# A kernel of attention and two MLPs: three narrow chunks beside attention in place of five, and groups of two steps with one tile

## The chip, the cores and the metric

The kernel runs on one core of a Trainium2 chip. The time is the device time of one execution in microseconds (us), the median of three runs; lower is better. Before the change it is 940.36 us (940.23 to 940.99).

## The reference

Three stages follow each other. `x` is the attention's output with the heads side by side, 2304 tokens of 512 values.

```python
# attention with random features: q, k, v (4, 8, 576, 64), omega (128, 64)
def phi(x):
    h = x @ omega.T - sum(x*x)/2          # x scaled before
    h = h - max(h)
    return exp(h) / sqrt(m)
kv  = phi(k).T @ v                         # per head, 128 x 64
z   = sum of phi(k)
out = (phi(q) @ kv) / (phi(q) @ z + 1e-6)
# first MLP: w_in (512, 2048), w_out (2048, 512)
h = x @ w_in
x = (max(h, 0) + alpha * min(h, 0)) @ w_out
# second MLP: w_a, w_b (512, 1536), w_out (1536, 512)
out = ((x @ w_a) * (x @ w_b)) @ w_out
```

## The kernel before

**Stages.** Attention runs in steps. A step takes a piece of 128 tokens (the last of a head group 64) of one group of four heads through its parts: projections `pp` of k and q on TensorE (a_proj), the maximum `nm` on VectorE (a_max), the exponential `ph` on ScalarE (a_exp), the state products `kv` (a_kv, with the copy `kvp` on ScalarE at the end of a head group, L838), the transposition `tp` of q's features and its copy `phT` (a_t, copied at L852 or on VectorE), the numerators `nd` with the reciprocals and quotients `xn` on VectorE (a_num), and the transposition `xp` of the output with its copy `xT` (a_x, at L894 or on VectorE). A part of a step comes some steps after the one it rests on, so that each step of the order holds parts of several pieces.

The first MLP is cut into 16 tiles of d_ff (128 each) in two phases of 8, and the tokens into chunks. A chunk's tile is 12 matmuls `h` (three for each of four slices of d_model, since every fp32 number is a high and a low part, xh and xl, wh and wl), the leaky relu with `u` and the parts `gh` on ScalarE and `gl` on VectorE, and 12 matmuls `y`. The chunks' inputs are split into xh (ScalarE, L517) and xl (L521). The second MLP, with a scheme that spares products (from 526.1 us), is not touched.

**What sets the order.** Every engine's order is written out by hand; a wait in an engine's queue holds all that is behind it. Steps 0 to 14 of attention run alone. From step 15 on (SPLIT_AT) narrow chunks of 256 tokens run beside attention, in the order of `work0`: chunks 0 and 1 in halves (tiles 0 to 4 of chunk 0, of chunk 1, tiles 5 to 7 of chunk 0, of chunk 1), then chunks 2, 3 and 4. At first A.run takes one tile and one step at a time. After ALONE = 4 entries of work0, which is from step 31 on, group() takes over: two steps and two tiles each. When attention has ended the rest of the narrow tiles run in pairs, then come the REST chunks, 512 wide, and the second phase.

Weights arrive packed and are decoded in pieces, through POOL, VectorE and ScalarE (L259 makes `r`, L308 the high part `w` from `a`). D_.step and D_.go set how many pieces stand at a place of the order.

**Banks and buffers.** PSUM has one bank for `kv`, five shared under the tag "ps" by pp, tp, nd, xp and the narrow tiles' h, and two for y. phT and xn have two buffers each, gh and gl three, u two; kvp three.

**Names.** On TensorE `y_256_0` is chunk 256 (its first token), half 0 of the output; `h_512_3` tile 3 of chunk 512; `pp(6, 1)_False` the projections of the keys of head group 6, piece 1 (and of a query's piece beside them; True means queries alone); `kv` a head group's state; `nd_4`, `xp_4`, `tp_4`, `phT_4` a piece 4 of some head group; the number behind is the tensor's own.

Of the kernel before, what the change touches and what calls it, by code (L numbers as in the profile page):

```python
# [23 lines left out]
KT = DM // P  # L24
# [8 lines left out]
WARM = 11  # L33
Q_LAG = 6
CI = 256
NCI = 5
NF0 = 8
NFH = 5
CB = 512
REST = (512, 512)  # L40
CHUNKS = (512, 512, 256, 512, 512)
NS = 25
NS1 = 17
# [9 lines left out]
DEC1 = 1.0  # L53
# [5 lines left out]
PACE2 = 1  # L59
PACE3 = 1  # L60
FIRST = 32
ALONE = 4
LAND = 5.0
SIDE = 0

# [2 lines left out]
def tile_kernel(ctx: ExitStack, tc: tile.TileContext, qT, kT, v1, omT, wbits, alpha, out):  # L68
# [58 lines left out]
    for ph in range(PH2):  # L127
        q = PB + QS * ph
        for j in range(2):
            f = 4 * ph + 2 * j  # L130
            for m in range(2):
                n = q + 7 * j + 3 * m
# [347 lines left out]
    class Mlp:  # L480
        def __init__(self, st, cap, ybufs, side=None):
            self.cap = cap
            self.pair = 2 * cap <= 512
            pool = lambda **kw: st.enter_context(tc.tile_pool(side=side, reuse_waits="tile" if side else "pool", **kw))

            if not self.pair:
                self.px = pool(name=f"px{cap}", bufs=6)
            self.xs, self.ys, self.gs, self.part = {}, {}, {}, {}
            self.half = {}
            self.q = []  # L490
            self.beside = None
            self.seen = set()
            self.after = []
            self.open_ = lambda: self.rest(pool, ybufs)
            if self.pair:
                self.open_()
# [104 lines left out]
        def a_back(self, ph, o, n, f, last_chunk):  # L601
# [23 lines left out]
                if i == end and not self.pair and e < 3 and not last:  # L625
                    D_.fill()
            D_.free[2 * f + 1] = last_chunk
            if last:
                if halves and f == NFH - 1:

                    yh = xT[:, :, 3 * S + o:3 * S + o + n]
                    for e in range(KT):
                        if e % 2:
                            vector.tensor_copy(yh[:, e], ys[e])
                        else:
                            nc.scalar.activation(yh[:, e], ys[e], AF.Copy)
                    self.half[o] = yh
                elif halves:
                    yo = self.half.pop(o)
                    for e in range(KT):  # L640
                        vector.tensor_tensor(out=yo[:, e], in0=ys[e], in1=yo[:, e], op=ALU.add)
                    nc.sync.dma_start(out=ypart[:, :, o:o + n], in_=yo)
                elif ph == 0:
                    yo = self.io.tile([P, KT, self.cap], F32, tag="io", name=f"yo{o}")[:, :, :n]
                    for e in range(KT):
                        if e % 2:
                            vector.tensor_copy(yo[:, e], ys[e])
                        else:
                            nc.scalar.activation(yo[:, e], ys[e], AF.Copy)
                    nc.sync.dma_start(out=ypart[:, :, o:o + n], in_=yo)  # L650
                else:
                    yp = self.part.pop(o)
                    for e in range(KT):
                        vector.tensor_tensor(out=yp[:, e], in0=ys[e], in1=yp[:, e], op=ALU.add)
                    nc.sync.dma_start(out=ypart[:, :, o:o + n], in_=yp)
                self.ys.pop(o)

        def load_y(self, o, n):
            yp = self.io.tile([P, KT, self.cap], F32, tag="io", name=f"yp{o}")[:, :, :n]
# [181 lines left out]
    def a_t(u, t):  # L841

        ns = slots_of(t)
        ph = phiq.pop((u, t))
        pp = bank(f"tp{u}_{t}").rearrange("p (o m) -> p o m", m=P)
        for h in range(ns):
            tensor.transpose(pp[:, h, :], ph[:, h, :], ident)
        d = pq.tile([P, 4, P], F32, tag="phT", name=f"phT{u}_{t}", bufs=2)
        if pick({"act": 0.1 + 0.13 * ns}, {"dve": 0.1 + 0.15 * ns}):
            vector.tensor_copy(d[:, :ns], pp[:, :ns])  # L850
        else:
            nc.scalar.activation(d[:, :ns], pp[:, :ns], AF.Copy)  # L852
        phT[u, t] = d
# [23 lines left out]
    def a_x(u, t, into=None):  # L877

        done["x"].add((u, t))
        b, g = divmod(u, HG)  # L880
        xn = xns.pop((u, t)).rearrange("p (a j) d -> p a (j d)", j=2)
        xp = (bank(f"xp{u}_{t}")[:, :256] if into is None else into).rearrange("p (a n) -> p a n", a=2)
        n = P if t < 4 else 64
        if t < 4:
            for a in range(2):
                tensor.transpose(xp[:, a, :], xn[:, a], ident)
        else:
            tensor.transpose(xp[:, 0, :], xn[:, 0], ident)
            xp = xp[:, 0, :].rearrange("p (a n) -> p a n", a=2)
        dst = xT[:, 2 * g:2 * g + 2, b * S + t * P:b * S + t * P + n]  # L890
        if pick({"act": 0.2 + n / 600}, {"dve": 0.1 + n / 480}):
            vector.tensor_copy(dst, xp)
        else:
            nc.scalar.activation(dst, xp, AF.Copy)  # L894
# [3 lines left out]
    done = {"kv": set(), "x": set()}  # L898
    late = {1: 3, 2: 3, 3: 4, 4: 5}
    own_banks = (0, 3, *range(6, SPLIT_AT, 2))  # L900
    held = {}
    for i, ut in enumerate((u, t) for u in range(U) for t in range(TT)):
        ev["k"][i] = ut
        ev["kv"][i + 1] = ut
# [110 lines left out]
    with st_m:  # L1015
# [38 lines left out]
        def group(fronts, at):  # L1054

            s = nxt_s[0]
            nxt_s[0] += 2
            D_.step(2 * DEC1)
            full = s < last_q
            todo = {n: wait[n][:2] for n in wait}  # L1060
            for n in wait:
                wait[n] = wait[n][2:]
            kv, t = list(todo["kv"]), list(todo["t"])
            for ut in todo["x"]:
                a_x(*ut)
            if kv:
                a_kv(*kv.pop(0))
            for ut in todo["num"]:
                a_num(*ut)
                wait["x"].append(ut)  # L1070
            if kv:
                a_kv(*kv.pop(0))
            spread(fronts, KT)
            A.flush()
            for x in (s, s + 1):
                pj = attn_1(x)
                loads(x)
                if pj:
                    a_exp(*pj, a_max(*pj))
                if x in ev["k"]:  # L1080
                    wait["kv"].append(ev["k"][x])
                if x in ev["q"]:
                    wait["t"].append(ev["q"][x])
            spread(line[at:at + 5], 2)
            D_.go(5)
            for i in range(2):
                if i < len(t):
                    a_t(*t[i])
                    wait["num"].append(t[i])
                if full:  # L1090
                    A.back_one(fronts, 2 - i)
            for w in fronts:
                A.whole(*w)
                if not full:
                    A.back_one(fronts)
            D_.go(3)

        def more():
            return nxt_s[0] < last_q or any(wait.values())
# [22 lines left out]
        def beside(ph, ci, i):  # L1122
# [13 lines left out]
            "num": [ut for ut in queries if ut in phT],  # L1136
            "x": [ut for ut in queries if ut in xns]})

        line = [(ph, o, n, f, lc) for ph, o, n, fs, lc in work0 for f in fs]

        def spread(fronts, most):
# [12 lines left out]
        while i < len(line):  # L1154
# [1 line left out]
                spread(line[i:i + 5], 2)  # L1156
            pair = []
            early = 1 if more() else 0
            for w in line[i:i + 2]:
                ph, o, n, f, _ = w  # L1160
                if all((ph, o, k) in A.xs or x_there(o + n, k, True) for k in range(KT)) and D_.ready >= 2 * f + 2 - early:
                    pair.append(w)
            if len(pair) < 2 and more():
                pair = []
            if more():
                group(pair, i)
            else:
# [6 lines left out]
        A.flush()  # L1174
        while more():
            group([], i)
        over()
        while A.q:
            A.pop()
# [338 lines left out]
```

## Time and profile before

| | |
|---|---|
| median of three runs | 940.36 us (940.23 to 940.99) |
| profiled execution, its own time | 941.56 us |
| its span in the profile | 939.8 us |
| TensorE (PE) busy | 928.4 us, 99% |
| VectorE (DVE) busy | 610.8 us, 65% |
| ScalarE (ACT) busy | 509.5 us, 54% |
| GpSimd (POOL) busy | 126.0 us, 13% |
| PE, h of the first MLP, first high part | 768 matmuls, 189.0 us |
| PE, y, first high part | 768 matmuls, 184.6 us |

The profile is of one execution. Its own time is 1.76 us over its span, and 1.2 us over the median of the runs. PE, DVE, ACT and POOL are the engines; PEld is TensorE's loading of weights, which goes on beside the matmuls. A time of day in the rows is counted in us from the start of the span. The first narrow tile begins at 41.0 us, and the last narrow chunk ends at 241.90 us. The granted clock is TensorE's, as a share of full speed.

### The profile page before, as it was taken

The numbers are of one execution on the slowest core, as the hardware profiler recorded it, in microseconds if no ns is written. First come the engines' busy times: TensorE is split into PE (matmuls) and PEld (weight loads), VectorE is DVE, ScalarE is ACT, GpSimd is POOL, SyncE is SP. The second block draws the span as 40 slices with busy tenths as digits, with TensorE's granted clock in tenths as the row PEclk, the third lists the DMA queues.
The fourth block names the chain that finished last, engine by engine and source line by source line (L and its number), as shares of the span: only waits on it lengthen the run. The fifth ranks groups of instructions, "written<-read, shape, count | busy, mean of one in ns | idle before, by whom it ended". The sixth has DMA issues, their size and how long they took to land.

```text
span 939.8 us, 16686 instructions
## 1 busy us (share of the span) xinstructions
PE 928.4 (99%) x6483; PEld 842.8 (90%) x6483; DVE 610.8 (65%) x1247; ACT 509.5 (54%) x1196; POOL 126.0 (13%) x107
## 2 busy tenths in 40 slices
PE   8899999999999999999999999999999999999998
PEld 7789999999888888889888999999999898989896
DVE  5988775644567677678676796866486833374633
ACT  7878865553455554455444555655456542444541
POOL 3677700000010201000000000000011111010201
PEclk9999999999999999999999999999999999999999
DMA  9354431000234242455555856269727368333323
GB/s 333 132 208 145 149 102 50 24 1 24 90 90 135 88 159 68 167 192 196 202 180 218 309 208 234 82 211 396 285 64 239 64 188 274 102 38 97 56 46 68
DMA packets 49566, 138.92 MB, mean 148 GB/s; under 512 B 4560, under 2 KB 11088, under 8 KB 49488
## 3 DMA queue, kind: packets, MB, share of 16 engines
q1 hardware_dynamic: 44592, 129.08, 38.6%
q0 software_dynamic: 4752, 8.65, 6.4%
q8 instruction: 51, 0.84, 0.3%
q14 instruction: 27, 0.22, 0.1%
q10 hardware_dynamic: 144, 0.13, 0.0%
HBM read 90.66 MB, written 47.19 MB: 147 GB/s over the span
## 4 chain that ended last, share of the span: by engine, by line
PE 95%; ACT 2%; DVE 2%; issue 0%; ACTq 0%; DVEq 0%
PE y L191 21%; PE h L191 21%; PE W L191 16%; PE o L191 16%; PE E L191 8%; PE B L191 4%; PE tp L191 2%; ACT ph L818 2%; PE kv L191 2%; PE nd L191 2%; PE xp L191 1%; DVE xl L521 0%; DVE a L191 0%; PE warm L191 0%; DVE xn L191 0%
## 5 line engine op out<-in xcount | busy, mean ns | idle before, releaser
L191 PE MATMUL h<-xh,w 128*128 128x256 f32 (+1 forms) x768 | 189.0, 338 | 0.4 <-DVE gl L191 0.4
L191 PE MATMUL y<-gh,w 128*128 128x256 f32 (+1 forms) x768 | 184.6, 339 | 0.0
L191 PEld LDWEIGHTS h<-xh,w 128*128 128x128 f32 x768 | 125.8, 190 | 16.0 <-DVE gl L191 0.6
L191 PEld LDWEIGHTS y<-gh,w 128*128 128x128 f32 x768 | 123.3, 189 | 15.1
L191 PE MATMUL o<-w,gh 128*128 128x512 f32 x432 | 133.2, 389 | 0.0
L191 PE MATMUL h<-xl,w 128*128 128x512 f32 (+1 forms) x384 | 109.9, 337 | 0.4 <-DVE xl L521 0.4
L191 PE MATMUL y<-gl,w 128*128 128x512 f32 (+1 forms) x384 | 109.5, 336 | 0.0
L191 PEld LDWEIGHTS o<-w,gh 128*128 128x128 f32 x432 | 81.0, 188 | 16.5
L191 DVE SCALAR_TENSOR_TENSOR h<-u,bend,h 128x512 f32<-128x512 f32 (+1 forms) x72 | 47.8, 663 | 56.9 <-ACT u L555 56.8
L191 PE MATMUL o<-w,gl 128*128 128x512 f32 x216 | 84.2, 390 | 0.0
L1417 POOL DMA_DIRECT2D out<-op x30 | 26.3, 877 | 421.9 <-ACT op L166 339.7
L567 ACT ACTIVATE gh<-h 128x512 fp32r<-128x512 f32 (+1 forms) x72 | 38.0, 527 | 64.7 <-DVE h L191 64.7
L191 PEld LDWEIGHTS h<-xl,w 128*128 128x128 f32 x384 | 64.3, 190 | 8.1 <-DVE xl L521 0.6
L191 PEld LDWEIGHTS y<-gl,w 128*128 128x128 f32 x384 | 64.1, 189 | 7.4
L555 ACT ACTIVATE u<-h 128x512 f32<-128x512 f32 (+1 forms) x72 | 38.1, 529 | 56.2 <-PE h L191 51.7
L521 POOL TENSOR_TENSOR xl<-xT,xh 128x512 fp32r<-128x512 f32 (+1 forms) x16 | 20.2, 1274 | 334.5 <-ACT xh L517 334.5
L166 ACT ACTIVATE u<-W 128x384 f32<-128x384 f32 x72 | 35.3, 492 | 50.6 <-PE W L191 47.3
L166 ACT ACTIVATE op<-o 128x512 f32<-128x512 f32 x51 | 30.4, 597 | 58.2 <-PE o L191 44.8
L191 DVE TENSOR_TENSOR u<-E,u 128x384 f32<-128x384 f32 x36 | 19.6, 555 | 52.5 <-PE E L191 49.7
L191 DVE TENSOR_TENSOR gl<-h,gh 128x512 fp32r<-128x512 f32 (+1 forms) x72 | 43.1, 599 | 15.4 <-ACT gh L567 14.6
L191 DVE CUSTOM_DVE_ANT_0 a<-a,r 128x1024 uint16<-128x1024 uint16 x68 | 49.1, 723 | 4.8 <-ACT r L259 0.8
L191 PEld LDWEIGHTS o<-w,gl 128*128 128x128 f32 x216 | 40.5, 188 | 8.4
(496 smaller groups left out, 1971.9 us busy)
## 6 DMA issues: line engine op xcount, KB each, us to landing
raw<-in_w SPq DMA_DIRECT2D x68, 512.0 KB, 5.1
w<-store SPq DMA_DIRECT2D x45, 512.0 KB, 6.9
store<-t_None SPq DMA_DIRECT2D x40, 512.0 KB, 3.6
st<-ypart SPq DMA_DIRECT2D x14, 768.0 KB, 7.4
out<-op POOLq DMA_DIRECT2D x30, 256.0 KB, 5.4
q<-in_qT SPq DMA_DIRECT2D x8, 576.0 KB, 3.8
v<-in_v SPq DMA_DIRECT2D x7, 650.0 KB, 6.2
yp<-ypart SPq DMA_DIRECT2D x4, 1024.0 KB, 6.3
```

The costliest lines, as they stand in the source:

```text
L166: nc.scalar.activation(out, in_, AF.Copy)
L191: return call(*a, **k)
L521: (nc.vector, nc.gpsimd)[way].tensor_tensor(out=lo, in0=src, in1=hi.bitcast(F32), op=ALU.subtract)
L555: nc.scalar.activation(u_, hp, AF.Relu, scale=-1.0)
L567: nc.scalar.activation(gh, hp, AF.Copy)
L818: nc.scalar.activation(ph[:, 2 * pr + j], pair[j][:, o + pr], AF.Exp, bias=nm[:, j, o + pr:o + pr + 1])
L1417: nc.gpsimd.dma_start(out=dst, in_=op, accum_op=ALU.add)
```

## The change

Of the nine narrow or wide chunks of the first phase, five of 256 and two of 512 tokens become three of 256 and three of 512. Groups begin after the first halves of chunks 0 and 1, with step 25, and hold two steps and one tile. Their parts are in another order, listed from the state products on: kv, nd, xp of both steps, the projections, then y of the tile before, then tp, then h. The maximum comes ahead of what A.flush emits (the rest of the tile before: gh and gl), the exponentials behind it. Within groups the copies phT are all on VectorE and the copies xT all on ScalarE; before, each was put where a running count of load was lower. The pieces of decoding (D_.go) stand behind tp and at the end, and D_.step is given one step's worth a group instead of two. The copies of a finished chunk's y out of PSUM are collected and emitted a little later (leave).

```diff
-NCI = 5
+NCI = 3
-REST = (512, 512)
+REST = (512, 512, 512)
-ALONE = 4
+ALONE = 2
...
@@ a_back
-            if last:
+
+            def leave():
                 if halves and f == NFH - 1:
...
+            if last:
+                self.outs.append(leave)
+                if not self.hold:
+                    self.leave()
+
+        def leave(self):
+            while self.outs:
+                self.outs.pop(0)()
+
@@ a_t
-        if pick({"act": 0.1 + 0.13 * ns}, {"dve": 0.1 + 0.15 * ns}):
+        if grouped or pick({"act": 0.1 + 0.13 * ns}, {"dve": 0.1 + 0.15 * ns}):
             vector.tensor_copy(d[:, :ns], pp[:, :ns])
@@ a_x
-        if pick({"act": 0.2 + n / 600}, {"dve": 0.1 + n / 480}):
+        if not grouped and pick({"act": 0.2 + n / 600}, {"dve": 0.1 + n / 480}):
             vector.tensor_copy(dst, xp)
@@ group
-            D_.step(2 * DEC1)
-            full = s < last_q
+            D_.step(DEC1)
             todo = {n: wait[n][:2] for n in wait}
             for n in wait:
                 wait[n] = wait[n][2:]
-            kv, t = list(todo["kv"]), list(todo["t"])
-            for ut in todo["x"]:
-                a_x(*ut)
-            if kv:
-                a_kv(*kv.pop(0))
+            for ut in todo["kv"]:
+                a_kv(*ut)
             for ut in todo["num"]:
                 a_num(*ut)
                 wait["x"].append(ut)
-            if kv:
-                a_kv(*kv.pop(0))
-            spread(fronts, KT)
-            A.flush()
+            for ut in todo["x"]:
+                a_x(*ut)
             for x in (s, s + 1):
                 pj = attn_1(x)
                 loads(x)
+                nm = a_max(*pj) if pj else None
+                A.flush()
                 if pj:
-                    a_exp(*pj, a_max(*pj))
+                    a_exp(*pj, nm)
...
-            spread(line[at:at + 5], 2)
-            D_.go(5)
-            for i in range(2):
-                if i < len(t):
-                    a_t(*t[i])
-                    wait["num"].append(t[i])
-                if full:
-                    A.back_one(fronts, 2 - i)
+            end = not (more() or todo["t"])
+            if not end:
+                A.back_one(fronts, 1)
+            for ut in todo["t"]:
+                a_t(*ut)
+                wait["num"].append(ut)
+            A.leave()
+            D_.go(3)
+            spread(fronts, KT)
             for w in fronts:
                 A.whole(*w)
-                if not full:
-                    A.back_one(fronts)
-            D_.go(3)
+                A.back_one(fronts)
+            A.leave()
+            spread(line[at:at + 5], 2)
+            D_.go()
...
-            for w in line[i:i + 2]:
+            for w in line[i:i + 1] if more() else line[i:i + 2]:
...
-            if len(pair) < 2 and more():
-                pair = []
```

Three places of the order are shown. The first is TensorE's queue where head group 5 ends and 6 begins. Before:

```order
L191 MATMUL kv_2005<-v_1587,ph_4_2275 64x65 x8
L191 MATMUL nd_1_2398<-kvp_169,phT_1_2310 64x65 x8
L191 MATMUL tp_0_2412<-ident,ph_0_2192 128x128 x4
L191 MATMUL y_256_0_2419<-gh_256_5_2174,w_89 128x256 x4
L191 MATMUL y_256_1_2420<-gh_256_5_2174,w_89 128x256 x4
L191 MATMUL y_256_0_2419<-gl_256_5_2175,w_89 128x256 x2
L191 MATMUL y_256_1_2420<-gl_256_5_2175,w_89 128x256 x2
L191 MATMUL xp_0_2433<-ident,xn_0_2303 128x128 x2
L191 MATMUL xp_1_2437<-ident,xn_1_2410 128x128 x2
L191 MATMUL kv_2441<-v_2088,ph_0_2379 64x65 x8
```

And after the change, the same place:

```order
L191 MATMUL kv_1994<-v_1587,ph_4_2213 64x65 x8
L191 MATMUL kv_2317<-v_2052,ph_0_2236 64x65 x8
L191 MATMUL nd_1_2326<-kvp_169,phT_1_2263 64x65 x8
L191 MATMUL nd_0_2340<-kvp_170,phT_0_2270 64x65 x8
L191 MATMUL xp_4_2354<-ident,xn_4_2172 128x128
L191 MATMUL xp_0_2357<-ident,xn_0_2186 128x128 x2
L191 MATMUL pp(6, 1)_False_2361<-xT,k_1886 128x128
```

The first product of the new head group (kv_2441 before, kv_2317 now) has moved up to directly behind the last of the old one.

The second is ScalarE's queue at the copy kvp_170 of the same place. Before:

```order
L567 ACTIVATE gh_256_7_2360<-h_256_7_2336 128x256
L818 ACTIVATE ph_0_2379<-pp(6, 0)_False_2362,nm(0, 6, 0)_2373 128x128 x2
L818 ACTIVATE ph_2_2380<-pp(6, 0)_False_2362,nm(0, 6, 0)_2373 128x128 x2
L818 ACTIVATE ph_0_2379<-pp(6, 0)_False_2363,nm(0, 6, 0)_2373 128x128 x2
L818 ACTIVATE ph_2_2380<-pp(6, 0)_False_2363,nm(0, 6, 0)_2373 128x128 x2
L838 ACTIVATE kvp_170<-kv_2005 128x260
L894 ACTIVATE xT<-xp_0_2433 128x2x128
L894 ACTIVATE xT<-xp_1_2437 128x2x128
```

After:

```order
L259 ACTIVATE r_2276<-raw_2120 128x512
L588 ACTIVATE u_0_7_2295<-h_0_7_2282 128x256
L518 ACTIVATE xh_512_0_2298<-xT 128x256
L518 ACTIVATE xh_512_1_2302<-xT 128x256
L308 ACTIVATE w_94<-a_2126 128x512
L849 ACTIVATE kvp_170<-kv_1994 128x260
L905 ACTIVATE xT<-xp_4_2354 128x2x64
L905 ACTIVATE xT<-xp_0_2357 128x2x128
L595 ACTIVATE gh_0_7_2374<-u_0_7_2295 128x256
```

In front of kvp_170 stood exponentials; now the u of a tile, two splits and a decoder's instruction stand there.

The third is ScalarE's queue in two of the last groups that hold attention. Before:

```order
L587 ACTIVATE u_1024_2_3860<-h_1024_2_3847 128x256
L587 ACTIVATE u_1024_3_3890<-h_1024_3_3877 128x256
L894 ACTIVATE xT<-xp_4_3905 128x2x64
L594 ACTIVATE gh_1024_2_3908<-u_1024_2_3860 128x256
L594 ACTIVATE gh_1024_3_3912<-u_1024_3_3890 128x256
```

After:

```order
L588 ACTIVATE u_512_4_3332<-h_512_4_3319 128x256
L905 ACTIVATE xT<-xp_3_3363 128x2x128
L905 ACTIVATE xT<-xp_4_3367 128x2x64
L595 ACTIVATE gh_512_4_3370<-u_512_4_3332 128x256
L588 ACTIVATE u_512_5_3404<-h_512_5_3391 128x256
L905 ACTIVATE xT<-xp_2_3417 128x2x128
L905 ACTIVATE xT<-xp_3_3421 128x2x128
L595 ACTIVATE gh_512_5_3425<-u_512_5_3404 128x256
```

Two tiles shared such a passage before, one tile has it to itself now, with two copies xT between its u and its gh.

## Rows read from the trace of the kernel before

**Rows 1.** The page: busy us (share of the span) xinstructions of each engine

```profile
PE 928.4 (99%) x6483; PEld 842.8 (90%) x6483; DVE 610.8 (65%) x1247; ACT 509.5 (54%) x1196; POOL 126.0 (13%) x107
```

**Rows 2.** TensorE's waits from 99 to 242: us in total, times, longest

```profile
PE tp L191 <- DVE xn L191: 0.2, 1, 0.2
```

**Rows 3.** Stretches: length, busy PE, PEld, DVE, ACT, POOL, clock, DMA share, GB/s

```profile
0.00:25.00 25.00, 21.90 (x297) 19.23 (x299) 14.07 (x38) 18.53 (x59) 9.29 (x12) 0.93 0.90 331
132.50:163.85 31.35, 31.35 (x414) 30.28 (x413) 18.80 (x50) 18.54 (x64) 0.00 (x0) 1.00 0.25 83
163.85:241.90 78.05, 77.78 (x870) 75.29 (x869) 39.85 (x120) 37.64 (x115) 0.00 (x0) 1.00 0.05 15
```

**Rows 4.** Timeline of TensorE: start, us, engine, operation, [idle before]; 24 matmuls twice

```profile
227.98 0.64 PE L191 MATMUL h<-xl,w 128*128 128x256 f32 x4
...
230.86 0.64 PE L191 MATMUL h<-xl,w 128*128 128x256 f32 x4
...
402.41 0.39 PE L191 MATMUL y<-gh,w 128*128 128x512 f32 x1
...
407.85 0.39 PE L191 MATMUL y<-gh,w 128*128 128x512 f32 x1
```

**Rows 5.** Timeline of TensorE: beginnings of pieces in steps 25 to 34

```profile
98.98 0.72 PE L191 MATMUL h<-xh,w 128*128 128x256 f32 x4
...
100.59 0.71 PE L191 MATMUL pp(5, 0)_False<-xT,k 64*128 64x128 f32 x8
...
132.53 0.60 PE L191 MATMUL xp<-ident,xn 128*128 128x128 f32 x4
...
142.88 0.69 PE L191 MATMUL kv<-v,ph 128*64 128x65 f32 x16
...
144.90 0.71 PE L191 MATMUL pp(6, 3)_False<-xT,k 64*128 64x128 f32 x8
...
146.66 0.66 PE L191 MATMUL tp<-ident,ph 128*128 128x128 f32 x4
147.07 1.19 PE L191 MATMUL y<-gh,w 128*128 128x256 f32 x8
...
148.58 0.38 PE L191 MATMUL tp<-ident,ph 128*128 128x128 f32 x2
...
153.11 0.60 PE L191 MATMUL xp<-ident,xn 128*128 128x128 f32 x4
153.64 0.69 PE L191 MATMUL kv<-v,ph 128*64 128x65 f32 x16
...
241.90 0.40 PE L191 MATMUL h<-xh,w 128*128 128x512 f32 x1
```

**Rows 6.** Timelines of ScalarE and TensorE: copies and what releases them

```profile
99.33 0.63 ACT L308 ACTIVATE w<-a 128x512 fp32r<-128x512 f32 x1 [0.21 <-DVE a L191]
...
99.87 0.37 ACT L852 ACTIVATE phT<-tp 128x256 f32<-128x256 f32 x1
...
172.37 0.84 ACT L517 ACTIVATE xh<-xT 128x256 fp32r<-128x256 f32 x2
...
185.46 0.69 PE L191 MATMUL kv<-v,ph 128*64 128x65 f32 x16
186.19 0.39 ACT L838 ACTIVATE kvp<-kv 128x260 f32<-128x260 f32 x1 [0.51 <-PE kv L191]
...
227.40 0.27 PE L191 MATMUL xp<-ident,xn 128*128 128x128 f32 x1
227.70 0.28 ACT L894 ACTIVATE xT<-xp 128x128 f32<-128x128 f32 x1 [1.17 <-PE xp L191]
...
231.82 1.12 PE L191 MATMUL y<-gh,w 128*128 128x256 f32 x8
232.02 0.38 ACT L587 ACTIVATE u<-h 128x256 f32<-128x256 f32 x1 [2.50 <-PE h L191]
232.95 0.42 ACT L594 ACTIVATE gh<-u 128x256 fp32r<-128x256 f32 x1 [0.24 <-DVE u L191]
```

More of the change, by code (lines that the diff above doesn't have):

```diff
@@ L493, in __init__ @@
             self.after = []
+            self.outs, self.hold = [], False
             self.open_ = lambda: self.rest(pool, ybufs)
@@ L900, in tile_kernel @@
     own_banks = (0, 3, *range(6, SPLIT_AT, 2))
-    held = {}
+    held, grouped = {}, []
     for i, ut in enumerate((u, t) for u in range(U) for t in range(TT)):
@@ L1137, in tile_kernel @@
             "x": [ut for ut in queries if ut in xns]})
+        grouped.append(True)
+        A.hold = True
         line = [(ph, o, n, f, lc) for ph, o, n, fs, lc in work0 for f in fs]
@@ L1176, in tile_kernel @@
             group([], i)
+        A.hold = False
         over()
```

## The prediction

> **What bounds the kernel now.** I read the page's busy times first: TensorE works 928.4 of 939.8 us [rows 1]. Its waits come second: between 99 us, where the first instruction moves, and 242 us, where the last narrow chunk has ended, TensorE waited 0.2 us in all [rows 2]. The table by stretch is third: TensorE fills 31.35 of 31.35 us and 77.78 of 78.05, at a granted clock of 1.00, while VectorE and ScalarE are at 60% in the one stretch (18.80 and 18.54 of 31.35) and at 50% in the other (39.85 and 37.64 of 78.05) [rows 3]. So in this part the time is the sum of what TensorE is given plus the waits that appear, and nothing can be won from the other engines. The timelines come last; I took pieces of TensorE's row as units [rows 4, 5] and ScalarE's copies between them as delays [rows 6].
>
> **What goes away.** Sixteen narrow d_ff tiles (two chunks of 256 tokens) become eight wide ones (one chunk of 512). A narrow tile has 24 matmuls of 128x256: from 227.98 to 230.86 is 2.88 us for 24 [rows 4]. A wide one has 24 of 128x512: from 402.41 to 407.85 is 5.44 [rows 4]. Sixteen times 2.88 is 46.1, eight times 5.44 is 43.5: 2.6 us less. These are durations of matmuls on a full engine, so the gain is of the path.
>
> The Trainium skill ("TensorE: Matmul & The Clock Gate", section "Back-to-back issue gap") gives the gap of two matmuls as their columns at 2.4 GHz plus 2.5 ns. By it the exchange would give an estimated 0.5 us (24 times 16 times 109.2 ns against 24 times 8 times 215.8), not 2.6. The rows show a pitch of 120 and of 227 ns, that is a surcharge of some 13 ns, five times the page's, so I keep them.
>
> **What the new groups take.** Attention has the same matmuls in both. Before, six single steps (25 to 30, with a tile each) run from 98.98 to 132.53, and a group of two steps with two tiles takes half of 132.53 to 153.11 [rows 5]; without its tiles that is 33.55/6 - 2.88 = 2.7 us a step and (20.58 - 4 x 2.88)/4 = 2.3 a step. I wrote out the new full group (two steps, one tile) with the pieces of [rows 5]: kv and nd of both steps 142.88 to 144.90, 2.02; xp 153.11 to 153.64, 0.53; the projections 144.90 to 146.66, 1.76; y 147.07 to 148.58, 1.51; a transposition of four 146.66 to 147.07, 0.41, of all 0.65; h 98.98 to 100.59, 1.6. Together 8.0 to 8.1. Fourteen groups follow step 25; the later ones hold less (the keys end, then the projections): 8.1 + 6 x 8.0 + 7.5 + 6.7 + 6.3 + 5.7 + 4.7 + 3.9 + 4.4 = 95.3. With the wide chunk's 43.5 that is 138.9, in place of 241.90 - 98.98 = 142.9 [rows 5]: **-4.0 us**. Of this 2.6 is the width and 1.4 the saved changes between kinds of work (137 stretches of one kind before, 88 after). Bounds of the second: nothing, if a change costs nothing, and 2.6, if all six single steps become as dear as those of a group (6 x 0.44).
>
> **What waits are added.** TensorE's order is fixed, so where a matmul stands too near to what it needs, everything behind it waits. I set the new order's distances on TensorE against the copies' delays.
>
> (a) The first group puts the numerators nd_4 next to the kv products, 0.5 us after 98.98. Their feature copy on ScalarE stands behind the decoder's hi (99.33, 0.63) and ends at 99.87 + 0.37 = 100.24 [rows 6]. With some 0.1 for the signal: **+0.8**. Bounds 0.5 and 1.0.
>
> (b) The kv products of both steps now stand back to back. Where head pair 5 ends and 6 begins, the second needs the one kv bank, which the copy kvp_170 must have emptied; on ScalarE that copy is behind u, two xh splits and a hi of the decoder. From the end of h: 0.20 (231.82 to 232.02) for the signal, u 0.38, the two splits 0.84, the hi 0.63, kvp 0.39 [rows 6]: 2.4, where TensorE comes at 0.5. Before, nd, transpositions and a y run stood between. **+1.9**, bounds 0.5 (the scheduler's splits came early) and 2.2.
>
> (c) State products first also means that nd, xp and the first projections follow each other closely. In eight groups the second bank of the first projection was last held by an xp, freed by its copy: the last transposition at +0.11, 0.30 to the copy (227.40 to 227.70), 0.39 for one of 256 columns (as kvp) [rows 6], so 0.8, where the projection starts 0.53 behind xp's start [rows 5]. 0.3 each; part is hidden, since the first of the two banks can be started. The same groups let xn's buffer wait for TensorE. **+1.8**, bounds 0 and 2.7.
>
> (d) In the group where (7, 0) begins, nd_0 needs kvp_169: kv's start to kvp's start is 0.73 (185.46 to 186.19), with 0.39 for it 1.1 [rows 6], and TensorE is there at 0.8. **+0.4**, bounds 0 and 0.6.
>
> (e) In the last three groups with attention there is little or no projection left between h and its y: nd, xp, a projection or none, y. TensorE is there 1.75, 1.45 and 0.9 us behind h's end. On ScalarE gh stands behind both xT copies, which wait for xp. u starts at 0.20 and takes 0.38; gh alone would start 0.93 behind u's start (232.02 to 232.95) [rows 6] and be done at 1.55, plus gl on VectorE later; with two copies of 0.39 ahead of it that cannot start before xp is through, it is 2.3, 2.4 and 1.85. Waits of 0.5, 0.95 and 0.95: **+2.4**, bounds 1.5 and 2.7. Before, two tiles were in work and the other one's matmuls lay between.
>
> (f) Smaller lacks behind the reduces (gl, maxima) in full groups: **+0.2**, bounds -0.2 and 2. VectorE gets all feature copies there, and I count 6 to 7.6 us of work for it in a group of 8.1: it is near, not over.
>
> The decoder's weight tiles are the same number in both and it stands at the same piece when the last chunk of the phase begins; from there on the order is the same, so I cost the rest at nothing. POOL is idle from 132.5 to 241.9 [rows 3], so its part of the decoding has room.
>
> **Sum.** -4.0 + 0.8 + 1.9 + 1.8 + 0.4 + 2.4 + 0.2 = +3.5 us on the profiled execution's 941.56 (span 939.8 and 1.76 around it), which gives 945.1. That execution lies 1.2 us over the median of the runs, 940.36; on the median the sum is 943.9. With all waits at their lower bounds (0.5 + 0.5 + 0 + 0 + 1.5 - 0.2 = 2.3) and -5.2 it is 937.5, with all at the upper (1.0 + 2.2 + 2.7 + 0.6 + 2.7 + 2 = 11.2) and -2.6 it is 949.
>
> **Rivals.** A change within 1.9 us (0.2%) can't be told from none here.
>
> No change: the scheduler's copies come early enough that (b), (c) and (d) are covered, since ScalarE is busy only 60%; (a) and (e) stay. -4.0 + 0.8 + 2.4 = -0.8: 939.6. For it: TensorE waited for nothing in this stretch before, with copies as near in many places [rows 2]. Against it: in (b) five instructions are ahead of the copy on its own engine, by order and not by chance.
>
> Faster, the other side: each change between kinds of work costs TensorE what the y run shows, 147.07 to 148.58 being 1.51 for 12 matmuls of 0.12 (1.44), so 0.07 [rows 5]. 49 fewer changes give 3.4 us, with the width 6.0; minus (a) and (e), 3.2, the time is 937.6. It decides from 0.04 a change on, if (b) and (c) together stay under 1 us. For it: six steps that ran singly cost 0.4 more each than in groups. Against it: the written-out group, whose pieces have their changes in them, gives back only 1.4.
>
> Much slower: VectorE becomes the bound in the full groups, since feature copies and reduces both go through it, and each of the eight takes 0.5 to 1 us more: +3.5 + 4 to 8, some 949. Against it: its share was 60% with half the feature copies [rows 3].
>
> The clock: TensorE was granted 0.93 in the first 25 us, when it was busy 21.90 of them, and 1.00 after it [rows 3]. Waits of 1 to 2 us in a stretch otherwise full leave it far busier than that. The Trainium skill ("TensorE: Matmul & The Clock Gate", Part 1, "The HAM clock gate") lets an idle engine fall to 1.2 GHz until it is busy again; by that rule a wait would cost twice what follows it for a while, which no row from 99 us on shows. I give it 2 in 100.
>
> **How the numbers follow.** Forecast with all waits 0.50, much slower 0.06, the clock 0.02, no change 0.22, faster 0.20; of the forecast's own chance 0.03 ends within 0.2%. The range of the likeliest case alone is 942 to 946.5; the one that holds 8 in 10 reaches into the faster case, 937.2, and to 947.4. Slower means over 942.2, faster under 938.5: slower 0.55, same 0.25, faster 0.20.
>
> **What would show it.** Right: pitches of 120 and 227 ns as before; the first 512-wide h at 98.98 + 95.3 + 7.5 of waits, near 202 us; in the waits of TensorE kv on kvp some 2 us once, y on gh three times with 2.4 together, nd on the feature copy 0.8 once, projections on xT in several groups. The same distances as before from the second wide chunk on. Wrong: TensorE's waits under 2 us in all between 99 us and the first wide chunk (then the no-change case or the faster one holds, told apart by the length of a full group: 8.0, or 7.7 and less); VectorE over 90% in the groups (much slower); a granted clock under 1.00 there; or a difference that only begins behind 250 us, which would say that the decoder or the transfers moved after all.

## The result and the profile after

The changed kernel takes 948.07 us (median of 6 runs, 947.85 to 948.36) where the kernel before takes 940.36: a ratio of 1.008, interval 1.0069 to 1.009. It is 7.7 us slower; 3.5 were forecast, and 948.07 lies 0.7 us over the range. The profiled execution took 948.1 with a span of 946.0. Page part 1 of the changed kernel, to be held against [rows 1]:

```profile
PE 929.3 (98%) x6291; PEld 833.4 (88%) x6291; DVE 611.2 (65%) x1225; ACT 502.4 (53%) x1168; POOL 134.2 (14%) x113
```

TensorE has 192 matmuls less and is busy 0.9 us longer. Its waits in the changed kernel from 99 to 250 us (in total, times, longest), where [rows 2] had one of 0.2:

```profile
PE y L191 <- ACT gh L595: 1.7, 2, 0.8
PE kv L191 <- ACT kvp L849: 1.6, 1, 1.6
PE y L191 <- ACT gh L568: 0.6, 1, 0.6
PE nd L191 <- ACT phT L863: 0.4, 1, 0.4
PE y L191 <- DVE gl L191: 0.2, 1, 0.2
```

That is 4.5 us, less than what is lost. The view lists only the longer waits (0.2 us is the shortest in it); the rest is in stretches that are a little longer each. So I summed TensorE's timeline by kind of work, each stretch from its first matmul to the first of the next kind, with the waits in it. It begins at the same y (97.34 before, 96.28 after) and ends at the first h of 512 columns (241.90 and 202.94):

| us | before | changed | outputs first | all mended |
|---|---|---|---|---|
| y | 49.23 (396 matmuls) | 26.30 (204) | 28.03 | 26.95 |
| h | 44.45 (360) | 22.28 (168) | 21.30 | 21.50 |
| pp (256) | 17.76 | 19.22 | 16.78 | 16.77 |
| kv (256) | 8.46 | 10.28 | 9.81 | 8.70 |
| nd (336) | 11.45 | 11.61 | 12.47 | 11.47 |
| xp (46) | 5.35 | 8.77 | 7.19 | 6.39 |
| tp (82) | 7.86 | 8.20 | 8.38 | 8.67 |
| all | 144.56 | 106.66 | 103.96 | 100.46 |

The tiles gave back 45.10 us (93.68 to 48.58). The same attention takes 58.08 where it took 50.88: 7.2 more. The wide chunk costs 43.52 when it runs on, and 1.36 more at its start (42.18 to the next chunk's first h, where the first wide chunk before took 40.83 for the same matmuls). -45.1 + 7.2 + 43.5 + 1.4 = 7.0. From the same y to the second MLP it is 436.00 against 428.81, that is 7.2: the 0.2 that the sum lacks is one short pause in a y of the second phase, at 442.1 us. From there to the end it is 413.72 against 413.66; so all of the loss is ahead of the second MLP.

The profiled execution of before had lost 1.06 us ahead of this place: it reaches the common y at 97.34 and the changed one at 96.28, and its granted clock in the first 25 us was 0.93 [rows 3], where the changed one has 1.00. That is nearly all of the 1.2 us by which it lay over the median, and it makes the difference of the two spans (6.2) smaller than that of the medians.

### The profile page after: what moved, and what is told of

It is laid out like the page before. It is cut to its first block, busy times and chain, and to the rows that moved or that the text cites. A ratio compares the mean times of both kernels' runs of the same rounds, so it can differ in the third digit from the quotient of the medians.

```text
span 946.0 us, 16214 instructions
## 1 busy us (share of the span) xinstructions
PE 929.3 (98%) x6291; PEld 833.4 (88%) x6291; DVE 611.2 (65%) x1225; ACT 502.4 (53%) x1168; POOL 134.2 (14%) x113
## 4 chain that ended last, share of the span: by engine, by line
PE 92%; ACT 4%; DVE 3%; issue 1%; DMA 0%; ACTq 0%
PE y L191 21%; PE h L191 20%; PE W L191 16%; PE o L191 16%; PE E L191 8%; PE B L191 4%; ACT ph L829 2%; PE nd L191 1%; PE tp L191 1%; PE kv L191 1%; PE xp L191 1%; DVE xl L522 1%; DMA ypart<-yo 0%; DVE a L191 0%; ACT phT L863 0%
## 5 line engine op out<-in xcount | busy, mean ns | idle before, releaser
L191 PE MATMUL h<-xh,w 128*128 128x512 f32 (+1 forms) x704 | 190.8, 353 | 0.4 <-DVE gl L191 0.4
L191 PE MATMUL y<-gh,w 128*128 128x512 f32 (+1 forms) x704 | 187.6, 353 | 2.3 <-ACT gh L595 1.7
L191 PEld LDWEIGHTS y<-gh,w 128*128 128x128 f32 x704 | 118.9, 188 | 22.3 <-ACT gh L595 2.6
L191 PEld LDWEIGHTS h<-xh,w 128*128 128x128 f32 x704 | 120.7, 189 | 18.6 <-DVE gl L191 0.6
L191 PE MATMUL y<-gl,w 128*128 128x512 f32 (+1 forms) x352 | 111.9, 351 | 0.2 <-DVE gl L191 0.2
L191 DVE SCALAR_TENSOR_TENSOR h<-u,bend,h 128x512 f32<-128x512 f32 (+1 forms) x74 | 50.9, 688 | 70.6 <-ACT u L556 70.6
L522 POOL TENSOR_TENSOR xl<-xT,xh 128x512 fp32r<-128x512 f32 (+1 forms) x22 | 28.0, 1282 | 324.6 <-ACT xh L518 324.6
L191 PEld LDWEIGHTS h<-xl,w 128*128 128x128 f32 x352 | 61.5, 189 | 9.3 <-DVE xl L522 0.6
L191 PEld LDWEIGHTS y<-gl,w 128*128 128x128 f32 x352 | 61.4, 189 | 9.4 <-DVE gl L191 0.7
L191 DVE TENSOR_TENSOR gl<-h,gh 128x512 fp32r<-128x512 f32 (+1 forms) x74 | 46.1, 624 | 20.9 <-ACT gh L568 20.0
```

The source lines that it names most:

```text
L191: return call(*a, **k)
L522: (nc.vector, nc.gpsimd)[way].tensor_tensor(out=lo, in0=src, in1=hi.bitcast(F32), op=ALU.subtract)
```

## The experiments

Each was timed in 5 rounds beside the kernel before. "Returned" is by how much the stretch from the common y to the second MLP is shorter than in the changed kernel, in the profiles, and so free of the clock's start; what comes behind the second MLP's beginning is not in it. The intervals of kv_apart, gh_first, y_behind_h, kvp_early and u_apart overlap with the changed kernel's, so for these five the profile and its waits carry the reading, and the median only agrees or doesn't.

| run | median us | ratio to before, interval | returned |
|---|---|---|---|
| changed kernel | 948.07 | 1.008 (1.0069 to 1.009) | |
| kv_apart | 947.0 | 1.0067 (1.0055 to 1.008) | 1.0 |
| x_first | 944.89 | 1.0044 (1.0032 to 1.0057) | 3.6 |
| gh_first | 948.07 | 1.0078 (1.0064 to 1.0091) | 1.3 |
| store_apart | 954.67 | 1.0148 (1.0134 to 1.0162) | 1.35 |
| y_behind_h | 946.07 | 1.0061 (1.0048 to 1.0074) | 2.0 |
| kvp_early | 946.99 | 1.0072 (1.0058 to 1.0086) | 1.1 |
| u_apart | 947.47 | 1.0074 (1.0061 to 1.0087) | 1.3 |
| all_mended | 940.3 | 1.0001 (0.9992 to 1.001) | 7.5 |
| old_group | 951.85 | 1.0119 (1.0105 to 1.0133) | -3.5 |
| copies_by_load | 949.79 | 1.0106 (1.009 to 1.0121) | -1.3 |
| mended_gl_first | 941.05 | 1.0004 (0.9995 to 1.0013) | 7.15 |
| h_beside_y | 946.55 | 1.006 (1.0047 to 1.0074) | 1.5 |

**State products apart, and kvp early.** Two ways at the same wait.

```diff
-            for ut in todo["kv"]:
+            for ut in todo["kv"][:1]:
                 a_kv(*ut)
             for ut in todo["num"]: ...
+            for ut in todo["kv"][1:]:
+                a_kv(*ut)
```

> The changed kernel, with the second state product of a group put behind the numerators again. Theory: the wait of the kv products for the copy kvp (a stretch of kv of 2.78 us where others take 0.98) is a cost of its own, because the copy runs while the numerators do; 1.5 to 1.8 us go, 946.2 to 946.6. Rival: the copy is late whatever stands between, and the numerators or the projections wait in its place; less than 0.5 us goes, over 947.6.

For the other, the two lines spread(line[at:at + 5], 2) and D_.go() move from a group's end to behind the next group's a_kv.

> The changed kernel, where the splits and decoding pieces at a group's end are emitted behind the next group's state products, so that on ScalarE the copy kvp comes right behind u. State products of both steps stay together. Theory: the stretch of kv of 2.78 us is long because of what stands before kvp on ScalarE (two splits, 0.77, and a high part, 0.67); with these behind, some 0.6 us of wait stays, since the copy can't be done sooner than 0.6 behind the product: 1.1 to 1.3 go, 946.8 to 947.0. Rival: the pieces of decoding and the splits, now later, are missed by the next h or y, so that nothing goes.

TensorE in the changed kernel at this place, and ScalarE beside it:

```profile
123.49 0.69 PE L191 MATMUL kv<-v,ph 128*64 128x65 f32 x16
125.75 0.69 PE L191 MATMUL kv<-v,ph 128*64 128x65 f32 x16 [1.58 <-ACT kvp L849]
```

```profile
123.87 0.42 ACT L588 ACTIVATE u<-h 128x256 f32<-128x256 f32 x1
124.14 0.77 ACT L518 ACTIVATE xh<-xT 128x256 fp32r<-128x256 f32 x2
124.75 0.67 ACT L308 ACTIVATE w<-a 128x512 fp32r<-128x512 f32 x1
125.27 0.43 ACT L849 ACTIVATE kvp<-kv 128x260 f32<-128x260 f32 x1
```

The product was done at some 124.0; its copy starts at 125.27, behind the splits and the decoder's w, in the order that was read off before. With kvp early the wait fell to 0.5:

```profile
PE kv L191 <- ACT kvp L849: 0.5, 1, 0.5
```

With the products apart it moved, since a numerator of the same group needs the same copy:

```profile
PE nd L191 <- ACT kvp L849: 1.1, 1, 1.1
```

So the copy's place in ScalarE's queue makes 1.1 of the 1.8 us by which the stretch of kv was longer, and another matmul in between is only part of a cover.

**Outputs first.**

```diff
+            for ut in todo["x"]:
+                a_x(*ut)
             for ut in todo["kv"]:
                 a_kv(*ut)
             for ut in todo["num"]: ...
-            for ut in todo["x"]:
-                a_x(*ut)
```

> The changed kernel, with the outputs' transpositions of a group ahead of the state products, as before the change; state products and numerators stay together. Theory: in the full groups the projections take 1.99 to 2.08 us, or 2.41, for 28 or 32 matmuls that took 1.76 and 1.99, because xp holds the bank that they need; with kv and nd between them this goes in eight groups, 1.8 to 2.6 us in all: 945.5 to 946.3, and 28 projections take 1.76. In the last groups xp would also be ready earlier, so that up to 1 us more goes. Rival: the banks of the numerators, which then stand right ahead of the projections, are freed as late; within 0.5 us of 948.1.

More than the theory asked for: 3.2 in the median, and in the profile 2.7 in the groups and 0.9 at the first wide chunk. The 0.9 is not shown to be the edit's: the store there was issued at the same place (2.2 us behind the first wide h) and ended 3.8 us later instead of 4.7. One full group on TensorE in the changed kernel, from its kv to its y:

```profile
133.67 1.15 PE L191 MATMUL kv<-v,ph 128*64 128x65 f32 x32
134.66 1.10 PE L191 MATMUL nd<-kvp,phT 128*64 128x65 f32 x32
135.69 0.66 PE L191 MATMUL xp<-ident,xn 128*128 128x128 f32 x4
136.28 0.92 PE L191 MATMUL pp(6, 3)_False<-xT,k 64*128 64x128 f32 x7
...
138.36 1.22 PE L191 MATMUL y<-gh,w 128*128 128x256 f32 x8
```

And with the outputs first:

```profile
133.55 0.60 PE L191 MATMUL xp<-ident,xn 128*128 128x128 f32 x4
134.08 1.15 PE L191 MATMUL kv<-v,ph 128*64 128x65 f32 x32
135.06 1.10 PE L191 MATMUL nd<-kvp,phT 128*64 128x65 f32 x32
136.09 0.71 PE L191 MATMUL pp(6, 3)_False<-xT,k 64*128 64x128 f32 x8
...
137.86 0.63 PE L191 MATMUL y<-gh,w 128*128 128x256 f32 x3
```

The projections take 1.77 instead of 2.08. In the changed kernel's trace the first of them in the second bank begins at 136.60, and the copy of xp that frees this bank ends at 136.55; the pause is too short for the list of waits. Beside that h is shorter by some 0.07 a group (22.28 to 21.30 us in the table, 14 stretches): a stretch of h that an xp follows lasted 1.52, one that a kv or nd follows 1.60 to 1.63. In the last groups y waited less for gh too. Against it stand a wait of 0.8 for xn in the first group and longer stretches of y, which now wait for gl.

**gh ahead of the copies, and y behind the next h.** First, in the last three groups:

```diff
+            if s >= last_q - 1:
+                A.flush()
             for ut in todo["x"]:
                 a_x(*ut)
```

> The changed kernel, where in the last three groups with attention gh and gl are emitted ahead of the outputs' copies xT. Theory: y waits there for gh, which stands behind two copies on ScalarE; of the 0.48, 0.95 and 0.96 us by which these stretches are longer 1.5 to 2.4 go: 945.7 to 946.6. Rival: u on VectorE sets gh's time, and the copies fill a gap that is there anyway; under 0.5 us goes, over 947.6.

Then, with the theory mended:

```diff
-            end = not (more() or todo["t"])
+            end = s >= last_q - 1
             if not end:
                 A.back_one(fronts, 1)
```

> The changed kernel, where from the group with the last projection on the y of a tile stands behind the h of the next tile. Theory, mended: there y follows its own h within 0.85 to 1.8 us, and the way from h over u, VectorE's part, gh and gl takes some 2 us by itself, whatever stands between on ScalarE; with another tile's h between, the stretches for y fall to 1.5 us and the xp before them to 0.5: of 2.1 us (0.48 + 0.9 + 0.96 over their length without a wait, less what is lost where the order meets the next) 1.6 to 2.3 go: 945.8 to 946.5. Rival: the waits move to the numerators, whose copies on VectorE then come as late; under 0.7 us goes.

TensorE and ScalarE of the changed kernel in such a group, then VectorE of the run with gh first in the same one:

```profile
190.07 1.22 PE L191 MATMUL y<-gh,w 128*128 128x256 f32 x8 [0.84 <-ACT gh L595]
187.77 0.38 ACT L588 ACTIVATE u<-h 128x256 f32<-128x256 f32 x1 [3.03 <-PE h L191]
189.16 0.55 ACT L905 ACTIVATE xT<-xp 128x256 f32<-128x256 f32 x2 [1.01 <-PE xp L191]
189.60 0.42 ACT L595 ACTIVATE gh<-u 128x256 fp32r<-128x256 f32 x1
```

```profile
187.92 0.48 DVE L191 SCALAR_TENSOR_TENSOR u<-u,bend,h 128x256 f32<-128x256 f32 x1 [1.05 <-ACT u L588]
188.32 0.15 DVE L191 TENSOR_SCALAR rc<-nd 128x4 f32<-128x4 f32 x1
...
190.04 0.41 DVE L191 TENSOR_TENSOR gl<-u,gh 128x256 fp32r<-128x256 f32 x1
```

In the changed kernel gh did stand behind the copies. Put ahead of them, it began 0.94 behind its u and not 1.83, but gl then stood behind two numerators' quotients on VectorE: the xp and y of that group together took 2.68 instead of 2.92. The median did not move (the profiled execution, 946.72, was the fastest of the five); of the 1.3 returned in the profile 0.7 lies in the groups, and 0.6 at the first wide chunk, which lost anything from 0.3 to 1.6 us in the runs that kept the buffers' places. With the next tile's h between, the waits of y for gh in the groups went, and 2.0 came back in profile and median. The place on ScalarE was the lesser half of the reason; the greater is that y follows its own h by 0.85 to 1.8 us.

**The first wide chunk.** TensorE and ScalarE in the changed kernel:

```profile
210.91 0.39 PE L191 MATMUL h<-xh,w 128*128 128x512 f32 x1
211.85 0.50 PE L191 MATMUL y<-gh,w 128*128 128x512 f32 x1 [0.55 <-ACT gh L568]
212.57 0.50 PE L191 MATMUL y<-gl,w 128*128 128x512 f32 x1 [0.22 <-DVE gl L191]
```

```profile
203.34 0.64 ACT L651 ACTIVATE yo<-y 128x256 f32<-128x256 f32 x2
209.78 0.60 ACT L556 ACTIVATE u<-h 128x512 f32<-128x512 f32 x1 [5.80 <-DMA ypart<-yo]
```

ScalarE sits 5.80 us before u, until the last narrow chunk's y has been stored: the wide chunk's buffers lie where it is stored from. SyncE issued this store (the changed kernel, then the kernel before, with the u that waited for it there):

```profile
205.10 0.51 SPq L652 DMA_DIRECT2D ypart<-yo  x1
```

```profile
243.06 0.51 SPq L650 DMA_DIRECT2D ypart<-yo  x1
246.82 0.60 ACT L555 ACTIVATE u<-h 128x512 f32<-128x512 f32 x1 [4.29 <-DMA ypart<-yo]
```

That is 2.16 us behind the first wide h (202.94) now and 1.16 before (241.90), and u began 6.84 and 4.92 behind it. Before, three y stood between the last narrow h and the first wide one; now two do, and VectorE comes 1.0 us later, counted from the wide h, to its copies of y. In h_beside_y, where three stand there again, the store was issued at 1.16 again. The other 0.9 lies in the store itself, which released u 3.8 us behind its issue before, 4.7 now, and 3.6 to 4.9 in the runs that kept the buffers' places; what sets this isn't shown. Two layouts were tried; store_apart has the y buffer first, u_apart only u ahead of gh and gl:

```diff
+            if not self.pair:
+                self.pu = pool(name=f"pu{cap}", bufs=1)
             self.pg = pool(name=f"pg{cap}", bufs=3)
-            self.pu = pool(name=f"pu{cap}", bufs=2 if self.pair else 1)
+            if self.pair:
+                self.pu = pool(name=f"pu{cap}", bufs=2)
```

> The changed kernel, with the buffers of the 512-wide chunks laid out in another order (the y buffer first), so that the first wide tile's u doesn't lie where the last narrow chunk's y is being stored from. Theory: u waits for that store (5.80 us idle until it), and this makes the first wide y late by 0.72 us and its matmuls by 0.63: 1.2 to 1.4 us go, 946.7 to 946.9. Rival: the lateness comes from ScalarE and VectorE, which still split the wide chunk's input when the last narrow y ends; under 0.3 us goes.

> The changed kernel with the buffer u of the wide chunks laid out ahead of gh and gl, and the y buffer at its place. Theory: the earlier layout run lost its time in the second MLP (one wait of 5.7 us of E for ScalarE's e), not at the first wide chunk, where its stretches were 8.19 and 2.72 as hoped; with the y buffer left in place the 1.2 to 1.4 us of the first wide chunk go and no wait comes later: 946.7 to 946.9. Rival: any shift of these buffers brings the wait in the second MLP; 950 or more.

In both u waited for its own h alone, began 2.95 us behind the first wide h, and the first y came in time (0.1 late in u_apart). The first lost 8.1 us behind the beginning of the second MLP: its trace has there, on ScalarE

```profile
ACT e L166 <- DMA ypart<-yp: 8.0, 1, 8.0
```

and on TensorE

```profile
PE E L191 <- ACT e L166: 5.7, 1, 5.7
```

The loss is longer than the wait, since the granted clock of TensorE, 1.00 up to the wait, was 0.50 (1.2 GHz) for some time behind its beginning, and 1.00 again while TensorE worked on; the table by stretch has (columns as in [rows 3])

```profile
541.20:547.80 6.60, 4.51 (x14) 4.51 (x15) 1.78 (x4) 3.80 (x9) 0.00 (x0) 0.50 0.02 6
```

There matmuls of 384 columns began every 0.32 us instead of every 0.17. The buffer moved from one store's way into another's. The second returned 1.3 in the profile; its median is only 0.6 lower, inside the intervals.

**All mended.** x first (not in the first group, and behind the state product where that ends a head group), kvp early, products apart, y behind h, u apart.

> The changed kernel with all of it: outputs' transpositions ahead of the numerators (but not in the first group, and behind the state product where that ends a head group), the second state product behind the first numerators, splits and decoding behind the first state product, y behind the next h in the last groups, and u laid out apart. Theory: the parts add up, 3.2 (x first) + 1.2 at the first group that x first lost + 1.6 (kvp) + 1.9 (y) + 1.3 (u) = 9.2 us of 948.1: some 939, that is the same as the kernel before or up to 1.5 us faster, since what is left are the two matmul terms. Rival: VectorE and ScalarE are so near to their limit in the groups that the waits only move; 942 to 944.

TensorE's waits from 90 to 260 us are then

```profile
PE nd L191 <- ACT phT L866: 0.4, 1, 0.4
```

940.3, no different from before. Of the 9.2 expected 7.8 came back, so the parts nearly add up, but what remains is nought and not the 4 us forecast as gain: the last column of the table still has 52.00 us for attention and 48.45 for tiles whose matmuls at 0.12 us are 44.64.

**One thing left: gl.**

```diff
+                A.flush()
                 nm = a_max(*pj) if pj else None
-                A.flush()
```

> The mended kernel of the run before, with gh and gl of the tile emitted ahead of the first maximum of a group. Theory: there y took 1.62 to 1.92 us in six groups, where 1.53 is its length, since gl stood behind a reduce of two times 0.64 us; 0.1 to 0.4 us go in each of these, 1.0 to 1.4 in all: 938.9 to 939.4, 0.1% under the kernel before. Rival: the maximum, now 0.35 later, delays the exponentials and with them the state products or transpositions by as much; 940 to 941.

y fell from 26.95 to 25.83 us, as meant; tp rose from 8.67 to 9.78 and pp by 0.37. The rival held: the wait was given back at the next use of what the maximum releases.

**Old order, and copies by load.** The first is the kernel before with NCI = 3, REST of three, ALONE = 2 and one tile a group; the second takes "grouped or" and "not grouped and" out of the two picks.

> The kernel before, with the changed one's three narrow and three wide chunks, groups from step 25 and one tile a group, but with the old order inside a group (outputs first, state products apart, gh and gl ahead of the maximum, tp ahead of y, decoding ahead of tp), the copies placed by the running count and y's copies at once. Theory: the loss is one of the new order, not of the widths nor of one tile a group; with the old order 940 to 942.5, where the wait at the first wide chunk (1.3) is still in it. Rival: a group with only one tile lacks cover whatever its order, or the changes between kinds of work cost what the width gives; 944 to 948.

> The changed kernel with the copies phT and xT placed by the running count of load again, all else as changed. Theory: where they stand costs or gives little, since the waits found were those of kvp, the banks, gh and the store, and of these only the copy xT moves to VectorE at places: 947 to 948.5. Rival: VectorE with all feature copies is what makes gl and the quotients late; 945 to 946.5.

Here my theory fell. The old order with one tile a group is slower than the changed kernel, by 3.8 us in the medians. Its waits from 90 to 260 us:

```profile
PE tp L191 <- ACT ph L818: 4.6, 7, 1.3
PE tp L191 <- DVE nm(0, 5, 3)_2093 L191: 2.3, 1, 2.3
```

Its transpositions take 18.00 us in all, where they took 7.86 before. Before, a y stood between the two of a group; with one tile it comes behind both, and the second follows right on the projections and waits for what their maxima and exponentials release. In the new order, with y ahead of tp, the transpositions take 8.20, with the copies at either place; y was not moved by itself.

Of the 3.8 us, 1.3 to 1.7 are the new place of the copies, by copies_by_load, which neither its theory nor its rival had foreseen. Some 1.5 more are the clock: behind the wait of 2.3 us, which ended at 115.08, the granted clock was 0.50 for a stretch in which TensorE was never idle,

```profile
115.80:119.10 3.30, 3.30 (x18) 3.30 (x17) 1.13 (x2) 3.30 (x12) 0.29 (x1) 0.50 0.02 5
```

and there a y took 2.49 us instead of 1.51 and an h 1.96 instead of 1.44. What is left for the order and the rest that differs is under 1 us.

**h beside y.** kv, nd and tp all ahead of the projections, h and y behind them.

> A third order of the group, with the mends of the wide chunk's u and of kvp: outputs, numerators, transpositions of the step before, state products (first where one ends a head group), both projections, then h and the y of the tile before side by side. Theory: a tile pays for its changes between kinds of work; with h and y adjacent y takes 1.44 in place of 1.53 and one change goes, so the two fall from 3.05 a group to 2.96, and no y can wait for gl, which in the mended kernel cost up to 0.39 in a group, 1.2 in all: 938.3 to 939.5. Rival: the cover behind the projections is what counts: with the transpositions moved away only h and y, 2.95 us, stand between a projection and the next use of its bank or its exponentials, where 3.9 stood; the numerators or state products wait 0.3 to 1 us in each of nine groups, 943 to 948.

The stretches became 1.53 and 1.44, as the theory had them, and the kernel lost 6 us against the mended one. In one of its groups:

```profile
115.13 0.69 PE L191 MATMUL nd<-kvp,phT 128*64 128x65 f32 x16 [0.33 <-ACT ph L832]
116.49 1.09 PE L191 MATMUL tp<-ident,ph 128*128 128x128 f32 x8 [0.67 <-DVE u L191]
```

Less stands between the projections and what needs their banks: the table's sum for nd is 14.23 (11.47 mended), for pp 19.70 (16.77), for tp 10.64 (8.67). The rival held: cover was worth more than fewer changes.

## Why the prediction was wrong

**Right:** where the loss would be, that TensorE's order against the copies would make it, the pitches of full stretches (0.120 and 0.227 us; the estimate of 215.8 ns by the formula in the Trainium skill, "TensorE: Matmul & The Clock Gate", section "Back-to-back issue gap", at 512 columns stands in no stretch here), that behind the second wide chunk next to nothing changes (0.2 us), and that neither the clock (1.00 from 25 us on) nor VectorE would be the bound. VectorE rose to 77% in the full groups (columns as in [rows 3]):

```profile
107.00:160.00 53.00, 51.42 (x777) 47.87 (x777) 41.01 (x106) 36.05 (x124) 9.92 (x7) 1.00 0.23 78
```

**The gain, -4.0, was some -1.6.** This is the first step that failed. The wide tiles took their 43.5, but the narrow ones gave back 45.1 and not 46.1, since the 14 that stayed each stand alone among other work (h 133 ns a matmul, 123 before; y 129, 124 before). The written-out group had this in its pieces: 14 h at 1.6 and 16 y at 1.51 make 46.6, and from the place that answers to 98.98 on they took 46.9. What was left of the -4.0 was a fall of attention from 50.8 to some 48.7 us without waits, by fewer changes between kinds of work, and that did not come: the stretches of one kind fell from 137 to 88, but with the waits mended attention still takes 52.00. From that place to the first wide h it took 105.0 us where 95.3 and 7.5 of waits were forecast, so 9.7 over the written-out groups. The full group itself was right where nothing stood in its way, with the outputs first 7.9 to 8.1 us for the 8.0 forecast in two of them; in the changed kernel every full group lies 0.3 us or more over. So much of what is missing is likely pauses too short for the list of waits, and not dearer pieces; one by one they were not traced.

**(c), +1.8, was at its upper bound.** With the outputs first the projections fell by 2.4 us and the groups by 2.7. The mechanism (the bank of xp) held; the size did not, because I took part of it as hidden.

**The wide chunk's start, not in the sum, was 1.4.** This is the second step that failed: I took the order there to be the same and costed the rest at nothing. In fact the last narrow chunk ends with one y less, the store was issued 1.0 us later and took 0.9 longer. It ended 6.4 us behind the start of the first copy of y, where it was 5.0 before; with three tiles' h as cover in both kernels, it came in time before and not now.

**(a)** was 0.6 of 0.8 (the numerators' wait 0.4). **(b)** was right: 1.8 of 1.9 by the stretch of kv. **(d)** was nothing new: that numerator's stretch was 1.27 before as well. **(e)** had the price, 2.0 for 2.4, but not the whole reason.

That attention's 7.2 more is near the 7.5 forecast as waits is luck, since attention was to fall by 2 apart from them; 6.1 of the 7.2 went with the mends and 1.1 stayed. The error (7.2 against 3.5 on the profiles) is 2.2 us up to the first wide h, 1.4 at its start and 0.2 in the second phase, but for 0.1 of rounding. The first wide h, forecast near 202 us, came at 202.94, but that is luck too: the changed kernel's profile reached the common y 1.06 us earlier, so on the time scale of the kernel before it came at 204.0.

The faster rival gave every change the same 0.07 us and had 3.4 us back from 49 fewer; the mended kernel has 35 fewer (102 stretches for 137) and the same time as the kernel before. The no-change rival had the copies of (b) and (c) early enough; their waits are in the trace. The rival of the clock did not occur in the changed kernel, whose longest wait was 1.6 us, but its argument reaches no further than waits of that size: in old_group a wait of 2.3 us was followed by a stretch at 0.50.

What stays open: why h is 0.08 longer ahead of kv than ahead of xp, and what the 52.00 us of attention in the mended kernel still hold above 50.88, beyond the listed waits; neither was tried by itself. Three narrow chunks with two tiles a group were not run either, so what the widths alone give, without the loss of cover, isn't shown.

## What to carry to other kernels

Where an engine is full and its order is written by hand, the work beside a chain is the chain's cover: taking half of it away, or moving it, brings back waits that no view of the kernel before shows, and a forecast has to ask of every neighbour what it needs and how long that takes from its own start. Price a change between kinds of work by the pair that meets, not by a mean. Ask of every buffer that is laid out anew which transfer still reads its place.

## What the runs showed that I had not expected

Laying out one buffer of the first MLP anew cost 8.1 us in the second, where an activation stood for 8.0 us behind a store. Of this 5.7 us were TensorE's wait, and the rest came behind it, while the granted clock was 0.50; in old_group too a wait was followed by such a stretch. The list of waits doesn't have this part of the price. The order that ran well with two tiles a group was the slowest but one with one tile (951.85). And a wait that was taken away on VectorE (y, 1.1 us) came back whole on the transpositions (1.1).
